# One transfer for wq, narrower last loads for w_up and w_down, and an up-row copy on ScalarE, in a decode layer on one core

## The chip, the cores and the metric

The kernel runs on one core of one Trainium2 chip. TensorE (PE) multiplies matrices, and PEld is its loading of stationary operands. VectorE (DVE) and ScalarE (ACT) do elementwise work, GpSimd (POOL) a little of it, and SyncE (SP) issues the loads. Loads move from device memory into the core's SBUF on 16 DMA engines. The metric is the device time of one execution in microseconds. Before the change it is 294.92 us, the median of three runs from 294.75 to 294.97 us.

## The reference, cut to what matters

Two tokens (batch 2, one position each, width 640) go through one transformer layer: a normalised attention over a cached window, then a gated feed-forward block, each with a residual.

```
x: [2,1,640]   k_cache, v_cache: [2,32,8192,192]   wq: [640,6144]   wo: [6144,640]
W = min(4096, max(256, 8192 // 4))                    # 2048
q = (layernorm(x) @ wq)   as 32 heads of 192
p = softmax(q . k_cache[:, :, 8192-W:, :] * 192**-0.5)
h = x + (p @ v_cache[:, :, 8192-W:, :]) @ wo
h2 = h + (gelu_tanh(layernorm(h) @ w_gate) * (layernorm(h) @ w_up)) @ w_down    # 640 -> 1536 -> 640
```

Everything is bf16 in memory. Only the last 2048 cached positions are read, which is 50.3 MB of K and as much of V, beside 7.9 MB each of wq and wo and 2.0 MB each of w_gate, w_up and w_down.

## The kernel before

**Operations and waits.** The kernel is written as a list of operations in program order. Each names the engine it runs on and the data it reads (`R`), writes (`W`) or shares a PSUM bank in (`X`). A helper then works out the semaphore waits from that list; each engine runs its own operations in exactly the listed order.

**Loads.** All large loads go through `load` and `pump` (L327 to L346) and are issued by SP at L342, in one fixed order: K of group 0, wq, K of group 1, V 0, K 2, V 1, K 3, V 2, K 4 and so on; wo in parts between; and at the end w_gate, w_up and w_down. They share one SBUF buffer, `ring`, of six slots of 24576 bytes per partition. A load may be issued when every earlier load whose bytes it overwrites has been used. SP issues in order, so a load that must wait also holds back those listed behind it. K group g lives in slot g % 4 and V group g in slot 4 or 5. At the start, wq borrows slots that K and V do not need yet: its three loads (`WQC`, 2, 2 and 1 of the five blocks of 128 rows) lie in slot 2, slot 3 and the first half of slot 5 (`WQ_AT`). Thus K 2 waits for the first wq load to be used, V 1 for the third, K 3 for the second; V 0, in slot 4, waits for nothing.

**Attention.** There are 16 groups; a group is four heads of one batch row, 3072 KB of K and 3072 KB of V. For each, TensorE transposes K (`transposes`, L549), DVE and ACT copy the result out (L561, L558), `scores` (L608) multiplies it by the query, `softmax` follows, and `pv` (L652) multiplies the weights by V. The order on TensorE is: transposes of group g, `pv` of group g-1, scores of group g. Before the first scores stand the transposes of K 0, then `q_rows` (L571), which computes the queries in 80 matmuls of 384 columns, 32 on the first wq load, 32 on the second and 16 on the third, then `q_stationary` (L589). After the groups come the last output projections (`oproj`, L703) and the second layer norm.

**Feed-forward.** `ffn_in` (L778) makes the 1536 gate values in 20 matmuls, four row strips of 384 columns side by side; `ffn_columns` copies these rows to `grow` on DVE (L785) and transposes them (L789). `h_rows` (L797) puts the residual into the output bank. DVE and ACT compute the gelu of the gate values (L807 to L814). The same two functions then make the up values from w_up; DVE multiplies both into `uT`; and 48 matmuls (L824), twelve on each of four w_down loads (`WDC`), add the result to the bank. It is copied to `yrow` (L830) and stored by two small transfers (L832).

Of the kernel before, what the change touches and what calls it, by code (L numbers as in the profile page):

```python
# [6 lines left out]
F32 = mybir.dt.float32  # L7
I32 = mybir.dt.int32
ALU = mybir.AluOpType
ACT = mybir.ActivationFunctionType  # L10
# [3 lines left out]
D = 640  # L14
NC5 = D // 128
HQ = 32
DH = 192
SKT = 8192
WIN = 2048
F = 1536  # L20
# [194 lines left out]
SLOT = 24576  # L215
RING = 6 * SLOT
TPG = 64
WQC = ((0, 2), (2, 4), (4, 5))
WDC = ((0, 3), (3, 6), (6, 9), (9, 12))
BIG = 1.0e9  # L220
K_AT = (0, SLOT, 2 * SLOT, 3 * SLOT)
V_AT = (4 * SLOT, 5 * SLOT)
WQ_AT = (2 * SLOT, 3 * SLOT, 5 * SLOT)
WO_AT = (3 * SLOT, 3 * SLOT, 2 * SLOT, 0)
WD_AT = (2 * SLOT + 15360, 2 * SLOT + 19200, 15360, 19200)


def bass_sequential_preLN__sliding_block_cached__geglu_ffn__decode_kernel(
# [12 lines left out]
    with ExitStack() as ctx:  # L241

        def sb(name, shape, dt):
            return ctx.enter_context(nc.sbuf_tensor(name, shape, dt))

        def ps(name, shape, dt):
            return ctx.enter_context(nc.psum_tensor(name, shape, dt))
# [5 lines left out]
        identf = sb("identf", [128, 128], F32)  # L253
# [31 lines left out]
        xnT = sb("xnT", [128, NC5, 136], BF16)  # L285
        hnT = sb("hnT", [128, NC5, B], BF16)
# [21 lines left out]
        hrow = sb("hrow", [128, 320], F32)  # L308
        hsel = sb("hsel", [128, 2, B], F32)
        grow = sb("grow", [128, 384], F32)  # L310
        gsb = sb("gsb", [128, NF * B], F32)
        ga = sb("ga", [128, 4, NF * B], F32)
        uT = sb("uT", [128, NF, B], BF16)

        tps = [ps(f"tps{i}", [128, 512], F32) for i in range(4)]
        sps = ps("sps", [128, 512], F32)
        ops_ = ps("ops", [128, 512], F32)
# [6 lines left out]
        where, live, queue, used = {}, [], [], set()  # L324

        def load(key, off, nbytes, src, shape, sem):
            queue.append((key, off, nbytes, src, shape, sem))  # L327

        def pump():
            while queue:  # L330
                key, off, nbytes, src, shape, sem = queue[0]
                old = [q for q in live if q[1] < off + nbytes and off < q[1] + q[2]]
                if any(q[0] not in used for q in old):
                    return
                for q in old:
                    live.remove(q)
                queue.pop(0)
                live.append((key, off, nbytes))
                v = shape(ring[:, off // 2:(off + nbytes) // 2])
                toks = [("ring", x) for x in range(off // GRAN, (off + nbytes + GRAN - 1) // GRAN)]  # L340
                where[key] = (v, toks)
                P.op("sp", lambda e, v=v, src=src: e.dma_start(v, src), W=toks + [("sem", sem)], dma=sem)  # L342

        def done(*keys):
            used.update(keys)
            pump()  # L346
# [9 lines left out]
            load(("v", g), V_AT[g % 2], SLOT, kv_src(A_v_cache, g), lambda v: v, f"v{g % 4}")  # L356

        def load_wq():
            wq = A_wq.rearrange("(p c) n -> p c n", c=NC5)
            for i, (c0, c1) in enumerate(WQC):  # L360
                load(("wq", i), WQ_AT[i], 2 * (c1 - c0) * HQ * DH, wq[:, c0:c1, :],
                     lambda v: v.rearrange("p (c n) -> p c n", n=HQ * DH), f"wq{i}")

        def load_wo(J):
            src = A_wo[1536 * J:1536 * (J + 1), :].rearrange("(p kk) n -> p kk n", kk=12)
# [5 lines left out]
            return ((0, 12),) if J < 3 else ((0, 8), (8, 12))  # L371

        def load_ffn():
            for key, at, w in (("wg", K_AT[1], B_w_gate), ("wu", K_AT[3], B_w_up)):
                load(key, at, 2 * NC5 * F, w.rearrange("(p c) f -> p c f", c=NC5),
                     lambda v: v.rearrange("p (c f) -> p c f", c=NC5), key)
            wd = B_w_down.rearrange("(r p j) n -> r p j n", p=128, j=3)
            for i, (f0, f1) in enumerate(WDC):
                load(("wd", i), WD_AT[i], 2 * (f1 - f0) * D, wd[i],
                     lambda v: v.rearrange("p (s n) -> p s n", n=D), f"wd{i}")  # L380


        def dve(fn, R=(), W=(), X=(), cls=1):
            return P.op("dve", fn, R, W, X, cls=cls)

        def act(fn, R=(), W=(), X=()):
            return P.op("act", fn, R, W, X)

        def pe(fn, R=(), W=(), X=()):
            return P.op("pe", fn, R, W, X)  # L390
# [10 lines left out]
        def tt(out, a, b, op):  # L401
            return lambda e: e.tensor_tensor(out=out, in0=a, in1=b, op=op)  # L402

        P.op("act", lambda e: e.dma_start(xrow[0:2, :], A_x[:, 0, :]), W=["xrow"], dma="dx")
        load_k(0)
        load_wq()
        load_k(1)
        for g in range(NG):
# [5 lines left out]
        load_wo(2)  # L414
        load_wo(3)
        load_ffn()
        pump()

# [42 lines left out]
        def _x_T(e):  # L461
# [11 lines left out]
            R=["pi"] + [("bits", k) for k in range(11)], W=["pti"])  # L473
# [87 lines left out]
                    dve(lambda e, dst=dst, bv=bv: e.tensor_copy(dst, bv), W=[("kt", n)], X=[("t", bi)], cls=0)  # L561

        def q_rows():
            for i, (c0, c1) in enumerate(WQC):
                wq, wtoks = where["wq", i]

                def fn(e, c0=c0, c1=c1, wq=wq):
                    for c in range(c0, c1):
                        for J in range(4):
                            for r in range(4):  # L570
                                ins = e.matmul(tps[0][32 * r:32 * (r + 1), 0:384], lhsT=xnT[:, c, 32 * J:32 * (J + 1)],  # L571
                                               rhs=wq[:, c - c0, 1536 * J + 384 * r:1536 * J + 384 * (r + 1)],
                                               start=(c == 0 and J == 0), stop=(c == NC5 - 1 and J == 3), tile_position=(0, 32 * r))
                    return ins

                pe(fn, R=["xnT"] + wtoks, X=[("t", 0)])
                done(("wq", i))
            act(lambda e: e.activation(
                out=qrow[:, :, :, :],
                in_=tps[0][:, 0:384].rearrange("p (h d) -> p h d", h=2).unsqueeze(2).to_broadcast([128, 2, 2, DH]),  # L580
                func=ACT.Copy, scale=SCALE), W=["qrow"], X=[("t", 0)])
# [147 lines left out]
        transposes(0, 0)  # L729
        transposes(0, 1)  # L730
        q_rows()
        q_stationary()
        consts_late()
# [35 lines left out]
        layernorm(m2[:, 32:42].rearrange("p (c b) -> p c b", b=B), [], ["m2"], hnT[:, :, :].unsqueeze(2), "hnT",  # L769
                  lambda e: e.matmul(m2[:, 16:18], lhsT=rs[0:98, :].to_broadcast([98, 128]), rhs=bsel[0:98, :], start=True, stop=True))  # L770

        def ffn_in(bank, xt, key):
            wv, wtoks = where[key]

            def fn(e):
                for c in range(NC5):
                    for r in range(4):
                        ins = e.matmul(bank[32 * r:32 * r + 2, 0:384], lhsT=hnT[:, c, :], rhs=wv[:, c, 384 * r:384 * (r + 1)],  # L778
                                       start=(c == 0), stop=(c == NC5 - 1), tile_position=(0, 32 * r))
                return ins  # L780

            pe(fn, R=["hnT"] + wtoks, X=[xt])

        def ffn_columns(bank, xt, i):
            dve(lambda e: e.tensor_copy(grow[0:98, :], bank[0:98, 0:384]), W=["grow"], X=[xt])  # L785

            def fn(e):
                for j in range(3):
                    ins = e.transpose(tps[i][:, 128 * j:128 * j + 98], grow[0:98, j:384:3], identf[0:98, 0:98])  # L789
                return ins  # L790

            pe(fn, R=["grow", "identf"], X=[("t", i)])
            return tps[i][:, 0:384].rearrange("p (j r y) -> p r j y", j=3, y=32)[:, :, :, 0:2]

        def h_rows(e):
            for r in range(4):
# [4 lines left out]
        def rjb(t):  # L801
            return t.rearrange("p (r j b) -> p r j b", r=4, j=3)

        ffn_in(sps, "s", "wg")
        gT = ffn_columns(sps, "s", 0)
        pe(h_rows, R=["hrow", ("hsel", 0), ("hsel", 1)], X=["m1"])
        dve(lambda e: e.tensor_copy(rjb(gsb[:, :]), gT), W=["gsb"], X=[("t", 0)])  # L807
        dve(tt(ga[:, 0, :], gsb[:, :], gsb[:, :], ALU.mult), R=["gsb"], W=["ga0"])
# [3 lines left out]
        dve(ts(ga[:, 3, :], ga[:, 2, :], 1.0, ALU.add), R=["ga2"], W=["ga3"])  # L812
        dve(lambda e: e.reciprocal(ga[:, 1, :], ga[:, 3, :]), R=["ga3"], W=["ga1"])
        dve(tt(ga[:, 0, :], ga[:, 1, :], gsb[:, :], ALU.mult), R=["ga1", "gsb"], W=["ga0"])  # L814
        ffn_in(ops_, "o", "wu")
        vT = ffn_columns(ops_, "o", 1)
        dve(tt(uT[:, :, :].rearrange("p (r j) b -> p r j b", r=4), vT, rjb(ga[:, 0, :]), ALU.mult), R=["ga0"], W=["uT"], X=[("t", 1)])
        for i, (f0, f1) in enumerate(WDC):
            wd, wtoks = where["wd", i]

            def fn(e, f0=f0, f1=f1, wd=wd):
                for f in range(f0, f1):
                    for r in range(4):
                        ins = e.matmul(m1[32 * r:32 * r + 2, 0:160], lhsT=uT[:, f, :],  # L824
                                       rhs=wd[:, f - f0, 160 * r:160 * (r + 1)], start=False, stop=(f == NF - 1),
                                       tile_position=(0, 32 * r), skip_group_check=True)
                return ins
# [3 lines left out]
        for b, q in ((0, "sp"), (1, "act")):  # L831
            P.op(q, lambda e, b=b: e.dma_start(out[b, 0, :].rearrange("(r n) -> r n", r=4), yrow[b:b + 97:32, :]),  # L832
                 R=["y"], W=[("out", b)], dma=f"dout{b}")
# [60 lines left out]
```

## Time and profile before

| what | value |
|---|---|
| median of three runs | 294.92 us |
| the profiled execution | 294.94 us, of which its span from first to last instruction is 293.0 us |
| TensorE busy, weight loads | 198.8 us, 153.0 us |
| VectorE, ScalarE, GpSimd busy | 128.5, 95.7, 8.4 us |
| mean granted TensorE clock | 0.834 of full speed |
| read from memory | 122.29 MB, 417 GB/s over the span |
| share of 16 DMA engines' time taken by SP's loads | 97.8% |
| a K load, issue to landing (median) | 32.7 us |

The span is cut in 40 slices of 7.3 us each for the busy rows. "Releaser" is what ended an engine's wait. A load's time from issue to landing includes the time it stands behind earlier loads.

### The profile page before, as it was taken

The numbers are of one execution on the slowest core, as the hardware profiler recorded it, in microseconds if no ns is written. First come the engines' busy times: TensorE is split into PE (matmuls) and PEld (weight loads), VectorE is DVE, ScalarE is ACT, GpSimd is POOL, SyncE is SP. The second block draws the span as 40 slices with busy tenths as digits, with TensorE's granted clock in tenths as the row PEclk, the third lists the DMA queues.
The fourth block names the chain that finished last, engine by engine and source line by source line (L and its number), as shares of the span: only waits on it lengthen the run. The fifth ranks groups of instructions, "written<-read, shape, count | busy, mean of one in ns | idle before, by whom it ended". The sixth has DMA issues, their size and how long they took to land.

```text
span 293.0 us, 5065 instructions
## 1 busy us (share of the span) xinstructions
PE 198.8 (68%) x2141; PEld 153.0 (52%) x2141; DVE 128.5 (44%) x311; ACT 95.7 (33%) x119; POOL 8.4 (3%) x35
## 2 busy tenths in 40 slices
PE   2573586858677298849493597659696869666764
PEld 1451264838474285628281575356666666533432
DVE  5950364433447045525264155415365435532332
ACT  2150144433442143616161144234343434520000
POOL 3000100000000000000000000000000000000000
PEclk9996569795979579998899599969797968997755
DMA  7999999999999999999999999999999999999993
GB/s 279 436 427 433 431 440 435 430 425 430 425 420 438 430 433 427 430 430 430 430 421 436 430 430 430 430 430 433 430 430 430 430 430 430 430 430 426 430 406 125
DMA packets 6654, 122.44 MB, mean 418 GB/s; under 512 B 754, under 2 KB 756, under 8 KB 1396
## 3 DMA queue, kind: packets, MB, share of 16 engines
q1 hardware_dynamic: 6632, 122.29, 97.8%
q8 instruction: 7, 0.11, 0.2%
q14 instruction: 3, 0.02, 0.0%
q10 hardware_dynamic: 12, 0.00, 0.0%
HBM read 122.29 MB, written 0.00 MB: 417 GB/s over the span
## 4 chain that ended last, share of the span: by engine, by line
DMA 72%; PE 23%; SPq 2%; DVE 2%; issue 1%; ACT 0%
DMA ring<-in_A_k_cache_dram 54%; PE tps L549 16%; DMA ring<-in_A_wq_dram 10%; DMA ring<-in_A_wo_dram 9%; SPq L342 2%; PE ops L652 1%; PE m L703 1%; PE m L824 1%; PE sps L778 1%; PE ops L778 1%; PE m L685 1%; PE tps L789 1%; PE tps L571 1%; PE m L722 0%; DVE grow L785 0%
## 5 line engine op out<-in xcount | busy, mean ns | idle before, releaser
L549 PE MATMUL tps<-identf,ring 128*128 128x128 f32 x768 | 116.5, 320 | 46.4 <-DMA ring<-in_A_k_cache_dram 45.5
L549 PEld LDWEIGHTS tps<-identf,ring 128*128 128x128 f32 x768 | 107.3, 168 | 49.8 <-DMA ring<-in_A_k_cache_dram 46.9
L558 ACT ACTIVATE ktr<-tps 128x1024 bf16<-128x1024 bf16 x80 | 79.4, 1023 | 87.4 <-PE tps L549 87.4
L561 DVE COPY ktr<-tps 128x1024 bf16<-128x1024 bf16 x112 | 74.0, 687 | 74.5 <-PE tps L549 73.8
L627 ACT ACTIVATE eexp<-sm,nm 128x512 bf16<-128x512 f32 x16 | 11.5, 721 | 64.5 <-DVE nm L625 64.5
L652 PE MATMUL ops<-ring,ering 128*32 128x384 bf16 x512 | 24.4, 334 | 4.7 <-DMA ring<-in_A_v_cache_dram 4.7
L608 PE MATMUL sps<-ktr,rq 128*16 128x512 bf16 x384 | 25.9, 404 | 1.1 <-POOL rq L402 1.1
L616 DVE CUSTOM_DVE_ANT_1 sm<-sps,mska 128x512 f32<-128x512 f32 x16 | 11.1, 691 | 34.9 <-PE sps L608 34.9
L652 PEld LDWEIGHTS ops<-ring,ering 128*32 128x32 bf16 x512 | 12.5, 97 | 13.0 <-DMA ring<-in_A_v_cache_dram 6.0
L608 PEld LDWEIGHTS sps<-ktr,rq 128*16 128x16 bf16 x384 | 9.4, 90 | 12.1 <-issue 2.1
L623 PEld LDWEIGHTS m<-mrhs,pm 128*128 128x128 bf16 x16 | 1.5, 96 | 22.8 <-DVE mrhs L398 22.8
L623 PE MATMUL m<-mrhs,pm 128*128 128x16 bf16 x16 | 2.9, 184 | 14.7 <-DVE mrhs L398 14.7
L402 POOL TENSOR_TENSOR rq<-qs,mask 128x96 bf16<-128x96 bf16 x16 | 5.6, 359 | 195.9 <-PE sps L608 164.9
L571 PE MATMUL tps<-ring,xnT 128*32 128x384 bf16 x80 | 5.7, 444 | 7.4 <-DMA ring<-in_A_wq_dram 7.3
L402 DVE TENSOR_TENSOR ering<-m,mask 128x256 bf16<-128x256 f32 x16 | 6.7, 418 | 3.6 <-PE m L636 3.6
L571 PEld LDWEIGHTS tps<-ring,xnT 128*32 128x32 bf16 x80 | 2.4, 120 | 10.3 <-DMA ring<-in_A_wq_dram 8.3
L454 ACT ACTIVATE lt<-m,eps_t 128x2 f32<-128x2 f32 x2 | 0.5, 262 | 20.1 <-PE m L452 20.1
L594 DVE CAST qs<-ops 128x384 bf16<-128x384 f32 x1 | 0.6, 558 | 14.4 <-PE ops L589 14.4
L636 PE MATMUL m<-sel,eexp 128*128 128x64 bf16 x64 | 5.3, 213 | 1.2 <-ACT eexp L627 1.2
L636 PEld LDWEIGHTS m<-sel,eexp 128*128 128x128 bf16 x64 | 4.9, 114 | 1.7 <-DVE nm L625 1.3
L703 PE MATMUL m<-ring,ot 128*2 128x320 bf16 x96 | 4.9, 338 | 1.1 <-DMA ring<-in_A_wo_dram 1.1
L402 DVE TENSOR_TENSOR orow<-m,wm 128x1536 bf16<-128x1536 f32 x3 | 5.3, 1750 | 0.0
(113 smaller groups left out, 84.2 us busy)
## 6 DMA issues: line engine op xcount, KB each, us to landing
ring<-in_A_k_cache_dram SPq DMA_DIRECT2D x16, 3072.0 KB, 32.7
ring<-in_A_v_cache_dram SPq DMA_DIRECT2D x16, 3072.0 KB, 27.6
ring<-in_A_wq_dram SPq DMA_DIRECT2D x2, 3072.0 KB, 21.0
ring<-in_A_wo_dram SPq DMA_DIRECT2D x3, 1920.0 KB, 19.4
ring<-in_B_w_gate_dram SPq DMA_DIRECT2D x1, 1920.0 KB, 30.9
ring<-in_B_w_up_dram SPq DMA_DIRECT2D x1, 1920.0 KB, 27.0
ring<-in_B_w_down_dram SPq DMA_DIRECT2D x4, 480.0 KB, 28.9
ring<-in_A_wq_dram SPq DMA_DIRECT2D x1, 1536.0 KB, 27.9
```

What stands on the lines that cost most here:

```text
L342: P.op("sp", lambda e, v=v, src=src: e.dma_start(v, src), W=toks + [("sem", sem)], dma=sem)
L402: return lambda e: e.tensor_tensor(out=out, in0=a, in1=b, op=op)
L549: ins = e.transpose(tps[bi][:, 128 * u:128 * (u + 1)], kv[:, off:off + 128], identf[:, :])
L558: act(lambda e, dst=dst, bv=bv: e.activation(out=dst, in_=bv, func=ACT.Copy), W=[("kt", n)], X=[("t", bi)])
L561: dve(lambda e, dst=dst, bv=bv: e.tensor_copy(dst, bv), W=[("kt", n)], X=[("t", bi)], cls=0)
L571: ins = e.matmul(tps[0][32 * r:32 * (r + 1), 0:384], lhsT=xnT[:, c, 32 * J:32 * (J + 1)], rhs=wq[:, c - c0, 1536 * J + 384 * r:1536 * J + ...
L608: ins = e.matmul(sps[32 * ch:32 * ch + 16, :], lhsT=rq[:, g % 4, k, :], rhs=ktr[:, k // 2, 1024 * ch + k % 2:1024 * (ch + 1):2], start=(k ...
L616: dve(lambda e: e.tensor_tensor_reduce(out=sm[:, :].rearrange("p (u x) -> p u x", u=4), in0=sps[:, :].rearrange("p (u x) -> p u x", u=4), ...
L627: act(lambda e: e.activation(out=eexp[:, :], in_=sm[:, :], func=ACT.Exp, bias=nm[:, 0:1], scale=1.0, accum_out=zr[:, g % 4:g % 4 + 1]), R= ...
L636: ins = e.matmul(o, lhsT=eexp[:, 128 * u:128 * (u + 1)], rhs=sel64[:, :], start=True, stop=True)
L652: ins = e.matmul(ops_[32 * r:32 * (r + 1), 0:384], lhsT=ering[:, g % 4, t, :], rhs=vv[:, 384 * t:384 * (t + 1)], start=(g % 4 == 0 and t < 4),
L703: ins = e.matmul(m1[32 * r:32 * r + 2, 192:512], lhsT=ot[:, kk, :], rhs=wo[:, kk - k0, 320 * h:320 * (h + 1)], start=(kk == 1 or J < 2 and ...
```

## The change

It has three parts.

- wq comes in one load, with 60 KB (61440 bytes) per partition, at the start of slot 2. It covers slots 2, 3 and the first half of slot 4. `q_rows` is one operation of 80 matmuls that waits for the whole of wq.
- w_up comes in two loads, four of its five blocks and then one (`WUC`), with 16 and 4 matmuls on them; and the last of the four w_down loads becomes two, with 8 and 4 matmuls on them. The bytes stay where they were.
- The rows of up values are copied out of PSUM by ScalarE into a new buffer `urow`; the gate rows stay with VectorE and `grow`.

```diff
-WQC = ((0, 2), (2, 4), (4, 5))
-WDC = ((0, 3), (3, 6), (6, 9), (9, 12))
+WDC = ((0, 3), (3, 6), (6, 9), (9, 11), (11, 12))
+WUC = ((0, 4), (4, 5))
-WQ_AT = (2 * SLOT, 3 * SLOT, 5 * SLOT)
+WQ_AT = 2 * SLOT
-WD_AT = (2 * SLOT + 15360, 2 * SLOT + 19200, 15360, 19200)
+WD_AT = (2 * SLOT + 15360, 2 * SLOT + 19200, 15360, 19200, 19200 + 2560)
...
+        urow = sb("urow", [128, 384], F32)
...
         def load_wq():
-            wq = A_wq.rearrange("(p c) n -> p c n", c=NC5)
-            for i, (c0, c1) in enumerate(WQC):
-                load(("wq", i), WQ_AT[i], 2 * (c1 - c0) * HQ * DH, wq[:, c0:c1, :],
-                     lambda v: v.rearrange("p (c n) -> p c n", n=HQ * DH), f"wq{i}")
+            load("wq", WQ_AT, 2 * NC5 * HQ * DH, A_wq.rearrange("(p c) n -> p c n", c=NC5),
+                 lambda v: v.rearrange("p (c n) -> p c n", n=HQ * DH), "wq")
...
         def load_ffn():
-            for key, at, w in (("wg", K_AT[1], B_w_gate), ("wu", K_AT[3], B_w_up)):
-                load(key, at, 2 * NC5 * F, w.rearrange("(p c) f -> p c f", c=NC5),
-                     lambda v: v.rearrange("p (c f) -> p c f", c=NC5), key)
+            load(("wg", 0), K_AT[1], 2 * NC5 * F, B_w_gate.rearrange("(p c) f -> p c f", c=NC5),
+                 lambda v: v.rearrange("p (c f) -> p c f", f=F), "wg")
+            for i, (c0, c1) in enumerate(WUC):
+                load(("wu", i), K_AT[3] + 2 * c0 * F, 2 * (c1 - c0) * F, B_w_up.rearrange("(p c) f -> p c f", c=NC5)[:, c0:c1, :],
+                     lambda v: v.rearrange("p (c f) -> p c f", f=F), f"wu{i}")
             wd = B_w_down.rearrange("(r p j) n -> r p j n", p=128, j=3)
             for i, (f0, f1) in enumerate(WDC):
-                load(("wd", i), WD_AT[i], 2 * (f1 - f0) * D, wd[i],
+                r = f0 // 3
+                load(("wd", i), WD_AT[i], 2 * (f1 - f0) * D, wd[r][:, f0 - 3 * r:f1 - 3 * r, :],
                      lambda v: v.rearrange("p (s n) -> p s n", n=D), f"wd{i}")
...
         def q_rows():
-            for i, (c0, c1) in enumerate(WQC):
-                wq, wtoks = where["wq", i]
...
-                pe(fn, R=["xnT"] + wtoks, X=[("t", 0)])
-                done(("wq", i))
+            wq, wtoks = where["wq"]
+
+            def fn(e):
+                for c in range(NC5):
+                    for J in range(4):
+                        for r in range(4):
+                            ins = e.matmul(tps[0][32 * r:32 * (r + 1), 0:384], lhsT=xnT[:, c, 32 * J:32 * (J + 1)],
+                                           rhs=wq[:, c, 1536 * J + 384 * r:1536 * J + 384 * (r + 1)],
+                                           start=(c == 0 and J == 0), stop=(c == NC5 - 1 and J == 3), tile_position=(0, 32 * r))
+                return ins
+
+            pe(fn, R=["xnT"] + wtoks, X=[("t", 0)])
+            done("wq")
...
-        def ffn_in(bank, xt, key):
-            wv, wtoks = where[key]
...
+        def ffn_in(bank, xt, key, parts):
+            for i, (c0, c1) in enumerate(parts):
+                wv, wtoks = where[key, i]
+
+                def fn(e, c0=c0, c1=c1, wv=wv):
+                    for c in range(c0, c1):
+                        for r in range(4):
+                            ins = e.matmul(bank[32 * r:32 * r + 2, 0:384], lhsT=hnT[:, c, :], rhs=wv[:, c - c0, 384 * r:384 * (r + 1)],
+                                           start=(c == 0), stop=(c == NC5 - 1), tile_position=(0, 32 * r))
+                    return ins
+
+                pe(fn, R=["hnT"] + wtoks, X=[xt])
...
-        ffn_in(ops_, "o", "wu")
-        vT = ffn_columns(ops_, "o", 1)
+        ffn_in(ops_, "o", "wu", WUC)
+        act(lambda e: e.activation(out=urow[0:98, :], in_=ops_[0:98, 0:384], func=ACT.Copy), W=["urow"], X=["o"])
+        vT = ffn_columns(urow, "urow", tps[1], 1)
```

The gate path keeps its copy on DVE; that copy now stands outside `ffn_columns`, which only transposes.

More of the change, by code (lines that the diff above doesn't have):

```diff
@@ L563, in q_rows @@
         def q_rows():
-            for i, (c0, c1) in enumerate(WQC):
-                wq, wtoks = where["wq", i]
[L567 to L574, printed above, removed]
-                pe(fn, R=["xnT"] + wtoks, X=[("t", 0)])
-                done(("wq", i))
+            wq, wtoks = where["wq"]
[9 more added lines that the diff above has]
+            done("wq")
             act(lambda e: e.activation(
@@ L770, in bass_sequential_preLN__sliding_block_cached__geglu_ffn__decode_kernel, with ffn_columns @@
                   lambda e: e.matmul(m2[:, 16:18], lhsT=rs[0:98, :].to_broadcast([98, 128]), rhs=bsel[0:98, :], start=True, stop=True))
-        def ffn_in(bank, xt, key):
-            wv, wtoks = where[key]
[L775 to L785, printed above, removed]
+        def ffn_in(bank, xt, key, parts):
[8 more added lines that the diff above has]
+                pe(fn, R=["hnT"] + wtoks, X=[xt])
+        def ffn_columns(row, tok, bank, i):
             def fn(e):
                 for j in range(3):
-                    ins = e.transpose(tps[i][:, 128 * j:128 * j + 98], grow[0:98, j:384:3], identf[0:98, 0:98])
+                    ins = e.transpose(bank[:, 128 * j:128 * j + 98], row[0:98, j:384:3], identf[0:98, 0:98])
                 return ins
-            pe(fn, R=["grow", "identf"], X=[("t", i)])
-            return tps[i][:, 0:384].rearrange("p (j r y) -> p r j y", j=3, y=32)[:, :, :, 0:2]
+            pe(fn, R=[tok, "identf"], X=[("t", i)])
+            return bank[:, 0:384].rearrange("p (j r y) -> p r j y", j=3, y=32)[:, :, :, 0:2]
         def h_rows(e):
@@ L802, in rjb @@
             return t.rearrange("p (r j b) -> p r j b", r=4, j=3)
-        ffn_in(sps, "s", "wg")
-        gT = ffn_columns(sps, "s", 0)
+        ffn_in(sps, "s", "wg", ((0, NC5),))
+        dve(lambda e: e.tensor_copy(grow[0:98, :], sps[0:98, 0:384]), W=["grow"], X=["s"])
+        gT = ffn_columns(grow, "grow", tps[0], 0)
         pe(h_rows, R=["hrow", ("hsel", 0), ("hsel", 1)], X=["m1"])
```

## Prediction

> **What bounds the kernel now.** I read the busy rows of the page first, then its chain of work, then the chain in order of time, then the timelines of both ends. The page:
>
> ```profile
> DMA  7999999999999999999999999999999999999993
> ...
> q1 hardware_dynamic: 6632, 122.29, 97.8%
> ...
> DMA 72%; PE 23%; SPq 2%; DVE 2%; issue 1%; ACT 0%
> ```
>
> The DMA row is full in all slices but the first and last: the loads bound the kernel, and a pause in them cannot be made up later. TensorE has room: it waits for K before 14 of the 16 groups (45.5 us in all).
>
> The chain in order of time, at the start:
>
> ```profile
> 2.53 27.89 DMA ring<-in_A_wq_dram
> 30.46 1.50 PE tps L571 x14
> 31.98 0.54 SPq L342
> 32.56 34.38 DMA ring<-in_A_k_cache_dram
> 66.99 5.38 PE tps L549 x24
> ```
>
> The last third of wq lands just before 30.46 us, its 16 matmuls run, and only then SP goes on. The timeline there:
>
> ```profile
> 3.71 0.65 SPq L342 DMA_DIRECT2D ring<-in_A_v_cache_dram  x1
> ...
> 18.96 1.49 PE L571 MATMUL tps<-ring,xnT 128*32 128x384 bf16 x32
> 20.49 0.54 SPq L342 DMA_DIRECT2D ring<-in_A_k_cache_dram  x1
> ...
> 26.77 2.75 PE L571 MATMUL tps<-ring,xnT 128*32 128x384 bf16 x32 [6.32 <-DMA ring<-in_A_wq_dram]
> ...
> 30.46 1.47 PE L571 MATMUL tps<-ring,xnT 128*32 128x384 bf16 x16 [0.95 <-DMA ring<-in_A_wq_dram]
> ...
> 52.38 4.35 PE L549 MATMUL tps<-identf,ring 128*128 128x128 f32 x24 [2.24 <-DMA ring<-in_A_k_cache_dram]
> ```
>
> V 0 is issued at 3.71 and K 2 at 20.49, so when SP is held until 31.98 two or three loads are still queued. K 2 is waited for until 52.38 and K 3 until 66.99, two loads later: 7.3 us per load of 3072 KB. The 32 matmuls took 1.49 us at full clock (46.6 ns each) and 2.75 us at the half clock after 20 us (86 ns each).
>
> The timeline at the end:
>
> ```profile
> 284.26 0.71 PE L797 MATMUL m<-hrow,hsel 98*2 98x160 f32 x8
> ...
> 284.93 0.10 PEld L778 LDWEIGHTS ops<-ring,hnT 128*2 128x2 bf16 x8 [0.56 <-DMA ring<-in_B_w_up_dram]
> ...
> 286.75 0.56 DVE L785 COPY grow<-ops 98x384 f32<-98x384 f32 x1 [0.53 <-PE ops L778]
> ...
> 289.67 0.23 PEld L824 LDWEIGHTS m<-ring,uT 128*2 128x2 bf16 x12 [0.24 <-DMA ring<-in_B_w_down_dram]
> ```
>
> Both waits are short: the arithmetic and the last loads arrive together.
>
> **What the Trainium skill says.** "DMA: Bandwidth & Descriptors", section "Why a DMA increments its semaphore by 16 and not by 1": the engines of a load finish independently, each adding one increment, and only all 16 mean landed. The trace agrees: the increments of wq's third load come at 28.6 to 29.0 us from fourteen engines, at 29.8 and 30.4 from two stragglers; those of K 1 from 35.9 to 37.7, of V 0 from 43.25 to 45.0. "TensorE: Matmul & The Clock Gate", section "What's actually happening": the array runs at half clock until about 3.4 us of sustained work, in a free-running window. Here the transposes ran slow for 3.3 us from 52.38 and for 5.4 us from 66.99.
>
> **Part one, wq.** V 0 lies in slot 4, which wq now covers, so SP waits before V 0 until all 80 query matmuls are done. Behind V 0 on SP stand K 2, V 1, K 3; ahead of it only K 1 is queued. K 1 is 7.3 us of transfer, and in that time the 80 matmuls must end and V 0 be started from an empty queue.
>
> - wq whole: its bytes and place in the stream are unchanged. At worst all increments are there at 30.4 as before; without the later straggler (one of the few instruction fetches, at 23.9 us, sits before it, and may move) at 29.8. I take 30.1.
> - 80 matmuls: TensorE has been idle since 18.9 us, so they begin at half clock. All slow is 80 x 86 ns = 6.9 us. With the clock rising after 3.3 us, 38 are slow and 42 take 46.6 ns: 5.3 us; after 5.4 us, 63 and 17: 6.2 us. I take 5.8. Already-warm would be 3.7. SP then issues about 0.1 us later, at 36.0 (30.1 + 5.8 + 0.1).
> - An unqueued load: K 0 is issued at 0.74, its increments come from 10.32 to 10.75, hence 9.6 to 10.0 us. V 0's first increments come at 36.0 + 9.6 = 45.6, against 43.25: most engines lose 2.35 us. A straggler loses less, 36.0 + 10.0 - 45.0 = 1.0 us.
> - What counts at the end is who finishes last. The increments of w_down's last load come from half the engines by 288.1, from six at 289.1 to 289.3 and from one at 289.6. As only two trailed at wq, most of the six fell back later and carry 2.35 us over: 289.3 + 2.35 = 291.65. The last landing moves by 291.65 - 289.6 = **+2.05 us**.
>
> Later stages shift with the stream. `scores` of group 0 and all behind it start about 4 us later, but `pv(0)` waits for V 0 anyway, and V 2 and K 4, issued after it near 49 us, have K 2, V 1 and K 3 queued ahead to about 68. TensorE's 2.2 to 3.2 us of wait per group take up the rest. One load instead of three saves SP 1.1 us of issuing at 2 us, under K 0's transfer: nothing. Longer rows: I take the same rate, since rows of 24 KB run at the same 430 GB/s as the rest; a per cent of 18.3 us would be 0.2 us either way.
>
> **Part two, w_up and w_down.** `h_rows`' last matmuls start by 284.5 and TensorE could go on at about 284.65, but w_up lands near 284.9. Its first four fifths land 384 KB earlier (0.9 us), and 16 matmuls cover the rest: 0.28 us. For w_down, twelve matmuls from 289.67 take 0.57 us; with a last load of four, all starting together, one matmul's 0.34 us remains: 0.23 us saved after the last landing, of which 44 earlier matmuls must be finished. Two more loads mean two more issues on SP (0.43 us each), at 258 us, when it has idle time until 290, and short rows: I charge 0.05 us. The issue of the last w_down load stood 4.8 us (until 264.5) before; two more such stalls still end well before the data's turn near 287.
>
> **Part three, ScalarE copy.** "ScalarE: Activation LUTs", section "What ACT_TABLE_LOAD costs": 186 ns + 0.833 ns per element, an estimate of 0.51 us for 384. The trace agrees on another tile: 768 elements should be 0.83 us, and L578 took 0.81. DVE took 0.558: 0.05 us saved. ScalarE is idle from 285.45, and the function is one already in use.
>
> **Sum.** w_up and the copy would bring `uT` 0.33 us forward, which only lets the w_down matmuls be ready for the last landing; the gain counted is w_down's 0.23 - 0.05 = 0.2 us. Thus +2.05 - 0.2 = +1.85 us on the profiled execution's 294.94, whose span would be 293.0 + 1.85. It lies 0.02 us from the median, so 294.92 + 1.85 = **296.8 us**.
>
> **Rivals.**
>
> - *Only the stragglers' loss counts* (the pause realigns the engines, and no new lag comes after it): +1.0 - 0.2 = +0.8, 295.7 us. For it: two engines do trail at wq. Against: six others trail at the end. Chance 0.15.
> - *The longer pause*: wq as late as 30.4 and the clock low for all 80: issue at 37.4, 1.4 us later than taken, 298.2 us. For it: in 26.77 to 29.52 and 30.46 to 31.98 the clock stayed at half. Against: transposes never ran slow over 5.4 us. Chance 0.17.
> - *No pause, the tail decides* (the other side): fourteen engines' landing at 29.0 sets the start and the array is warm, 3.7 us, so that V 0 is issued at 32.8, before 43.25 - 9.6 = 33.65. Then the tail's 0.2 to 0.35 us remain, 294.6 us. It is not slower than noise for an issue up to about 34.8 (pause 1.1 us). Against: half clock throughout 25 to 30 us. Chance 0.07.
> - *Mine*: 0.61.
>
> **Numbers.** A change under 0.2% (0.6 us, 294.33 to 295.51) can't be told from none. From the cases: slower 0.90, same 0.08, faster 0.02. The likeliest case alone spans 296.0 to 297.7 (wq 29.8 to 30.4, matmuls 5.3 to 6.2). The range 295.6 to 298.2 takes in the first two rivals and leaves the third out.
>
> **What would show it.** V 0 issued near 36 us after a wait on L571's 80 matmuls, a dent in the DMA row's fifth or sixth slice, K 2 waited for about 1 to 2.5 us later, and K 15 likewise. At the end: no wait before w_up's matmuls, four matmuls after the last landing, a ScalarE copy near 0.5 us. I am wrong if V 0 is issued by 34.5, if wq's landing moves by over 1 us, or if the end keeps less than the pause.

## The result and the profile after

The changed kernel takes 296.43 us (median of five runs, 296.24 to 296.80) against 294.92 us for the kernel before (five runs, 294.54 to 295.04). The ratio is 1.0055, with a 95% interval from 1.004 to 1.007: slower by half a per cent, 1.5 us. The profiled execution took 296.34 us with a span of 294.2 us, against 294.94 and 293.0. The forecast was 296.8 us in a range from 295.6 to 298.2.

**The start.** The timeline of the changed kernel, TensorE and SP (start and duration in us; in square brackets the idle time before and its releaser):

```profile
29.71 4.70 PE L572 MATMUL tps<-ring,xnT 128*32 128x384 bf16 x80 [10.89 <-DMA ring<-in_A_wq_dram]
34.46 0.54 SPq L343 DMA_DIRECT2D ring<-in_A_v_cache_dram  x1
35.03 1.09 SPq L343 DMA_DIRECT2D ring<-in_A_k_cache_dram  x1
...
54.31 1.97 PE L551 MATMUL tps<-identf,ring 128*128 128x128 f32 x8 [3.47 <-DMA ring<-in_A_k_cache_dram]
```

All 80 query matmuls stand in one row after the landing of wq, and SP issues V 0 only behind them, at 34.46 us instead of 3.71. K 2 is now waited for until 54.31 us, 1.9 us later than the 52.38 of before. The waits of SP name the new one: once, for 31.8 us, SP stood until TensorE had done the query matmuls.

```profile
SPq L343 <- PE tps L572: 31.8, 1, 31.8
```

What that does to the stream is seen in windows of 2 us. After the length come the busy times of PE, PEld, DVE, ACT and POOL with their counts of instructions, then the granted clock, the share of the DMA engines and, last, GB/s. The kernel before, then the changed one:

```profile
33.00:35.00 2.00, 0.87 (x16) 0.63 (x18) 1.25 (x5) 0.00 (x0) 0.64 (x2) 0.50 1.08 467
35.00:37.00 2.00, 2.00 (x24) 0.55 (x16) 1.90 (x10) 0.00 (x0) 0.74 (x3) 0.50 0.92 393
37.00:39.00 2.00, 0.92 (x10) 0.29 (x3) 1.46 (x6) 0.00 (x0) 0.35 (x1) 0.50 0.91 393
```

```profile
33.00:35.00 2.00, 1.41 (x36) 0.73 (x28) 0.00 (x0) 0.54 (x1) 0.00 (x0) 1.00 0.97 414
35.00:37.00 2.00, 0.55 (x16) 0.43 (x18) 1.11 (x4) 0.27 (x1) 0.46 (x2) 1.00 0.92 258
37.00:39.00 2.00, 1.52 (x24) 0.48 (x24) 1.90 (x9) 0.00 (x0) 1.28 (x4) 1.00 0.94 393
```

Between 35 and 37 us the changed kernel moves 258 GB/s where the one before moves 393. The share column does not move (0.92 in both). In the packet records the first packets of V 0 took 1.31 to 1.86 us on fourteen engines, where a packet of 24 KB in the full stream takes 0.91, and an engine counts as busy over the whole of such a packet. So here the bytes show the pause and the share does not.

**The end.** The timeline of the changed kernel:

```profile
285.55 0.71 PE L797 MATMUL m<-hrow,hsel 98*2 98x160 f32 x8
...
286.04 1.82 PE L780 MATMUL ops<-ring,hnT 128*2 128x384 bf16 x20
...
287.90 0.49 ACT L817 ACTIVATE urow<-ops 98x384 f32<-98x384 f32 x1 [1.16 <-PE ops L780]
...
290.90 0.10 PEld L826 LDWEIGHTS m<-ring,uT 128*2 128x2 bf16 x8 [0.39 <-DMA ring<-in_B_w_down_dram]
291.30 0.09 PEld L826 LDWEIGHTS m<-ring,uT 128*2 128x2 bf16 x4 [0.29 <-DMA ring<-in_B_w_down_dram]
291.65 0.33 DVE L832 CAST yrow<-m 98x160 bf16<-98x160 f32 x1 [2.22 <-PE m L826]
```

The up matmuls no longer wait for w_up, the ScalarE copy takes 0.49 us, and four matmuls follow the last landing. The chain that ended last, by parts, says the same of the whole. In the kernel before it leads back through wo and the arithmetic behind it, in the changed kernel through w_down's load. The kernel before, then the changed one:

```profile
DMA ring<-in_A_k_cache_dram 54%; PE tps L549 16%; DMA ring<-in_A_wq_dram 10%; DMA ring<-in_A_wo_dram 9%; SPq L342 2%; PE ops L652 1%; PE m L703 1%; PE m L824 1%; PE sps L778 1%; PE ops L778 1%; PE m L685 1%; PE tps L789 1%; PE tps L571 1%; PE m L722 0%; DVE grow L785 0%
```

```profile
DMA ring<-in_A_k_cache_dram 57%; PE tps L551 14%; DMA ring<-in_A_wq_dram 10%; DMA ring<-in_B_w_down_dram 8%; SPq L343 4%; PE tps L572 2%; PE ops L653 1%; DVE ktr L563 1%; ACT ktr L560 1%; PE m L704 1%; PE m L686 1%; DVE ering L404 0%; PE m L826 0%; PE m L667 0%; DVE yrow L832 0%
```

**The increments.** The trace also records each of the 16 increments of a load's semaphore. For V 0 and for the last load of w_down this table gives the first and the last (us); the spread is how far, in the last load, the last engine trails the first. The median time is that of all runs of the kernel, the increments are of its one profiled execution.

```
kernel            V 0 issued   V 0 first   V 0 last   last load: first    last   spread   median time
before               3.71        43.25       45.03        287.50         289.62    2.12      294.92
after               34.46        44.12       45.45        288.52         291.25    2.73      296.43
```

The first engines lose 0.87 us at V 0 and 1.02 us at the end. The last engine loses 1.63 us at the end. The difference of 0.61 us is a spread that has grown. From the last landing to the copy of the output row it was 0.67 us (289.62 to 290.29) and is 0.40 us (291.25 to 291.65), so the new end gives 0.27 us back. The sum is 1.02 + 0.61 - 0.27 = 1.36 us, against 1.40 us between the two profiled executions.

**The engine that lands last.** The packet records do not name the engine, but one engine's packets can be followed, since each begins within 0.02 us of the end of the one before. This is the engine whose V 0 lands last in the changed kernel (us):

```
start            took        size         what
36.90            1.48        24 KB        V 0, its first packet (thirteen other engines begin V 0 by 36.13)
38.38            1.27        24 KB        V 0
39.64 to 49.63   0.91 each   24 KB x11    the rest of V 0, then K 2
49.63            0.94        16 KB        an instruction fetch, on another queue (q8)
50.56            1.42        24 KB        K 2
```

At V 0 this engine trails the first by 1.33 us, where at K 1, just ahead of the pause, the last engine trailed by 1.68: the pause did bring the engines a little closer together. At K 2 it trails by 2.83 us, while the other fifteen lie within 0.75 us. The step of 1.5 us is the fetch and the slower load packet behind it. The kernel before has such a fetch at 49.41 us too, but there it meets one of the fourteen engines that lie within 0.4 us of the first, and the spread stays (1.78 us at V 0, 1.75 at K 2). In the changed kernel's last load, all engines but this one have landed by 290.51 us, 0.89 us after the 289.62 of before. So, by estimate, about 0.7 of the 1.63 us is a fetch that met the engine that was already last.

### The profile page after: what moved, and what is told of

The parts are those of the page before. It is cut to its first block, busy times and chain, and to the rows that moved or that the text cites. A ratio compares the mean times of both kernels' runs of the same rounds, so it can differ in the third digit from the quotient of the medians.

```text
span 294.2 us, 5066 instructions
## 1 busy us (share of the span) xinstructions
PE 193.8 (66%) x2141; PEld 151.1 (51%) x2141; DVE 128.2 (44%) x310; ACT 96.1 (33%) x120; POOL 8.4 (3%) x35
## 4 chain that ended last, share of the span: by engine, by line
DMA 75%; PE 18%; SPq 4%; DVE 1%; ACT 1%; issue 1%
DMA ring<-in_A_k_cache_dram 57%; PE tps L551 14%; DMA ring<-in_A_wq_dram 10%; DMA ring<-in_B_w_down_dram 8%; SPq L343 4%; PE tps L572 2%; PE ops L653 1%; DVE ktr L563 1%; ACT ktr L560 1%; PE m L704 1%; PE m L686 1%; DVE ering L404 0%; PE m L826 0%; PE m L667 0%; DVE yrow L832 0%
## 5 line engine op out<-in xcount | busy, mean ns | idle before, releaser
L551 PE MATMUL tps<-identf,ring 128*128 128x128 f32 x768 | 115.0, 318 | 47.8 <-DMA ring<-in_A_k_cache_dram 46.9
L551 PEld LDWEIGHTS tps<-identf,ring 128*128 128x128 f32 x768 | 106.1, 167 | 51.1 <-DMA ring<-in_A_k_cache_dram 48.2
L653 PE MATMUL ops<-ring,ering 128*32 128x384 bf16 x512 | 25.0, 339 | 4.7 <-DMA ring<-in_A_v_cache_dram 4.7
L617 DVE CUSTOM_DVE_ANT_1 sm<-sps,mska 128x512 f32<-128x512 f32 x16 | 11.1, 691 | 34.8 <-PE sps L609 34.8
L609 PE MATMUL sps<-ktr,rq 128*16 128x512 bf16 x384 | 24.7, 389 | 1.1 <-POOL rq L404 1.1
L572 PE MATMUL tps<-ring,xnT 128*32 128x384 bf16 x80 | 4.7, 407 | 10.9 <-DMA ring<-in_A_wq_dram 10.9
L579 ACT ACTIVATE qrow<-tps 128x768 bf16<-128x768 f32 x1 | 0.8, 810 | 14.6 <-PE tps L572 14.6
```

Of the source, the lines that this page charges most:

```text
L551: ins = e.transpose(tps[bi][:, 128 * u:128 * (u + 1)], kv[:, off:off + 128], identf[:, :])
L609: ins = e.matmul(sps[32 * ch:32 * ch + 16, :], lhsT=rq[:, g % 4, k, :], rhs=ktr[:, k // 2, 1024 * ch + k % 2:1024 * (ch + 1):2], start=(k ...
L617: dve(lambda e: e.tensor_tensor_reduce(out=sm[:, :].rearrange("p (u x) -> p u x", u=4), in0=sps[:, :].rearrange("p (u x) -> p u x", u=4), ...
L653: ins = e.matmul(ops_[32 * r:32 * (r + 1), 0:384], lhsT=ering[:, g % 4, t, :], rhs=vv[:, 384 * t:384 * (t + 1)], start=(g % 4 == 0 and t < 4),
```

## Experiments

The theory: the loss is a pause in the stream of loads, made where V 0 waits for the 80 query matmuls while only K 1 is left in the queue; the end gains a little. All ratios are to the kernel before. The rivals: the one wide load costs by itself; any late use of wq costs; the small loads at the end cost; the loss is partly absorbed.

**The first part alone.** Of the changed kernel only the wq part is kept:

```diff
-WDC = ((0, 3), (3, 6), (6, 9), (9, 11), (11, 12))
-WUC = ((0, 4), (4, 5))
+WDC = ((0, 3), (3, 6), (6, 9), (9, 12))
+WUC = ((0, 5),)
...
-        act(lambda e: e.activation(out=urow[0:98, :], in_=ops_[0:98, 0:384], func=ACT.Copy), W=["urow"], X=["o"])
+        dve(lambda e: e.tensor_copy(urow[0:98, :], ops_[0:98, 0:384]), W=["urow"], X=["o"])
```

> The change with its end undone: wq in one load at slots 2 to 4.5, but w_up in one load, w_down in four, and the up rows copied by VectorE. Pause theory (the whole loss is made at the start, where V 0 waits for the 80 query matmuls): V 0 issued at 34.3 to 35.5 us as in the changed kernel, its first increments near 44.1, and the end keeps it and lacks the 0.2 us of the new end, 296.4 to 297.0 us. Rival (the new small loads at the end cost something): faster than the changed kernel's 296.4, at 295.5 or less.

Measured: 295.99 us (seven runs, 295.46 to 296.74), ratio 1.0033 (1.0022 to 1.0044). The loss is there without the new end. But the median lies below the expected span and below the changed kernel's, and above what the rival asks for. So neither expectation holds as it was put: this kernel lacks the new end and still comes out 0.4 us faster than the changed one, though the intervals of the two ratios overlap. The runs lie 1.3 us apart, where those of the end alone (below) lie 0.5 us apart, so the 0.2 us of the new end cannot be read from this comparison. The profiled execution was the slowest of the seven, with V 0 issued at 35.23 us, as expected; its first increment came at 44.71, later than the 44.1 expected.

**The end alone.** wq, `q_rows`, `WQC` and `WQ_AT` are those of the kernel before:

```diff
+WQC = ((0, 2), (2, 4), (4, 5))
...
-WQ_AT = 2 * SLOT
+WQ_AT = (2 * SLOT, 3 * SLOT, 5 * SLOT)
...
```

> The end alone: wq in three loads as before, w_up in loads of 4 and 1, w_down's last block in 2 and 1, up rows copied by ScalarE. Pause theory: no loss, 0.1 to 0.4 us gained, 294.5 to 294.8 us; w_up's 20 matmuls start without a wait, four matmuls follow the last landing. Rival (small loads and two more issues delay the last landing): 295.2 us or more, with the last landing after 289.8 us.

Measured: 294.75 us (13 runs), ratio 0.9994 (0.9986 to 1.0003). That is within the expected span, but its interval includes no gain. Its one profile has a gain of 0.25 us: the last landing is where it was (289.64 after 289.62), the copy of the output row comes at 290.04 instead of 290.29. The small loads cost nothing that can be seen.

**V slots exchanged.** The one wide load stays, and all 80 query matmuls still wait for all of it; V 0 no longer lies under it:

```diff
-V_AT = (4 * SLOT, 5 * SLOT)
+V_AT = (5 * SLOT, 4 * SLOT)
```

> The changed kernel with the two V slots exchanged (V 0 in slot 5, V 1 in slot 4): wq is still one load of 60 KB rows and all 80 query matmuls still wait for it, but V 0 waits for nothing and K 2 is the first that waits. Pause theory: V 0 is issued near 3 us, K 2 near 34.5 us with V 0 still to come, so the stream has no pause: 294.3 to 294.9 us. Rival (the single wide load, or the late queries, cost the time by themselves): 296.2 to 296.8 us as in the changed kernel.

Measured: 294.54 us (21 runs, 294.22 to 294.93), ratio 0.9988 (0.9981 to 0.9994). This decides between the pause and the wide load. Its timeline of SP at the start and its window from 35 to 37 us:

```profile
2.65 0.60 SPq L343 DMA_DIRECT2D ring<-in_A_v_cache_dram  x1
...
35.78 0.53 SPq L343 DMA_DIRECT2D ring<-in_A_k_cache_dram  x1
```

```profile
35.00:37.00 2.00, 1.08 (x32) 0.61 (x24) 0.00 (x0) 0.81 (x1) 0.00 (x0) 1.00 0.93 393
```

The query matmuls end even later than in the changed kernel (SP goes on at 35.78 us), but it is K 2 that waits then, with V 0 still to be moved, and the stream runs on at 393 GB/s. With the same load and the same late queries the loss is gone, and with it the rival. This kernel is even faster than the kernel before, by 0.12%.

**Queries twice.** The 80 query matmuls are done twice, and the second pass restarts the accumulation:

```diff
-                for c in range(NC5):
+                for c in list(range(NC5)) * 2:
```

> The changed kernel with the 80 query matmuls done twice (the second pass restarts the accumulation, the output is the same). 80 more matmuls at full clock are 3.7 us more before V 0 is issued, near 38.2 us. Pause theory: all of it reaches the end, 299.6 to 300.5 us. Rival (what the start loses is partly absorbed by the 2 to 3 us of room in each group, or by realigned engines): under 298.5 us.

Measured: 299.0 us (four runs, 298.76 to 299.29), 2.6 us over the changed kernel: between the two expectations, so neither holds as it was put. The increments show where the rest went. V 0 is issued 3.89 us later (38.35), its first increment comes 3.68 us later (47.80), and the last load's first 3.73 us later (292.25): the pause reaches the end whole. But the last engine comes only 2.79 us later (294.04), since the spread at the end is 1.79 us instead of 2.73. At V 0 it is 0.48 us (47.80 to 48.28): in the longer pause all engines ran empty, and they restarted together. At K 2 an instruction fetch at 54.23 us puts one of them back, and the spread is 1.91 us; in the changed kernel a fetch in the same load met an engine that was 1.33 us late already. So part of the longer pause is given back, by realigned engines, as the rival said, but only 0.94 of 3.73 us.

**Three loads, but V 0 waits.** wq lies where the changed kernel has it, in three loads:

```diff
+WQC = ((0, 2), (2, 4), (4, 5))
...
-WQ_AT = 2 * SLOT
+WQ_AT = (2 * SLOT, 3 * SLOT, 4 * SLOT)
...
```

> The changed kernel's place of wq (slots 2, 3 and the first half of 4, so V 0 must wait) and its end, but wq again in three loads, with 32, 32 and 16 query matmuls on them. Pause theory: only 16 matmuls stand after the last landing, V 0 is issued near 32.0 us, before the 33.65 us from which a pause begins, so there is none: 294.4 to 295.0 us. Rival (that V 0 waits for wq at all costs the time): 295.8 us or more.

Measured: 294.75 us (13 runs), ratio 0.9996 (0.9988 to 1.0004), V 0 issued at 32.06 us. Waiting for wq costs nothing while the wait ends early enough. It is the 64 matmuls moved behind the last landing that make it late.

**The two halves of the end.** First only w_down's last load is cut, then only w_up is cut and the copy moved to ScalarE; wq is that of the kernel before in both. The diffs are against the kernel with the end alone. The first:

```diff
 WDC = ((0, 3), (3, 6), (6, 9), (9, 11), (11, 12))
-WUC = ((0, 4), (4, 5))
+WUC = ((0, 5),)
...
-        act(lambda e: e.activation(out=urow[0:98, :], in_=ops_[0:98, 0:384], func=ACT.Copy), W=["urow"], X=["o"])
+        dve(lambda e: e.tensor_copy(urow[0:98, :], ops_[0:98, 0:384]), W=["urow"], X=["o"])
```

> The kernel before with only w_down's last load cut in 2 and 1. Theory of the end (it is set by the last landing and the matmuls behind it): four matmuls instead of twelve after the last landing, but they queue behind the eight of the load ahead, so the copy of the output row starts 0.1 to 0.25 us earlier than 290.29; 294.6 to 294.9 us. Rival (the short load lands later): the copy starts at 290.29 or after.

The second:

```diff
-WDC = ((0, 3), (3, 6), (6, 9), (9, 11), (11, 12))
+WDC = ((0, 3), (3, 6), (6, 9), (9, 12))
```

> The kernel before with only w_up in loads of 4 and 1 and the up rows copied by ScalarE. Theory of the end: uT is ready 0.3 us earlier but twelve matmuls still wait for the last w_down load, so the copy of the output row starts within 0.1 us of 290.29; 294.8 to 295.0 us. Rival (the end is set by the chain of arithmetic): 0.3 us gained, 294.6 us, the copy at 290.0.

Measured: 294.77 us, ratio 0.9999 (0.9991 to 1.0007), and 294.88 us, ratio 1.0001 (0.9993 to 1.0009); neither can be told from no change. The timelines show what each does. Only w_down cut:

```profile
288.39 1.77 PE L830 MATMUL m<-ring,uT 128*2 128x160 bf16 x48 [0.28 <-DVE uT L407]
290.21 0.32 DVE L836 CAST yrow<-m 98x160 bf16<-98x160 f32 x1 [1.88 <-PE m L830]
```

Only w_up cut and the copy moved:

```profile
288.00 1.37 PE L830 MATMUL m<-ring,uT 128*2 128x160 bf16 x36 [0.27 <-DVE uT L407]
...
289.81 0.57 PE L830 MATMUL m<-ring,uT 128*2 128x160 bf16 x12 [0.45 <-DMA ring<-in_B_w_down_dram]
290.43 0.33 DVE L836 CAST yrow<-m 98x160 bf16<-98x160 f32 x1 [2.49 <-PE m L830]
```

In the first, the 48 matmuls run without a wait and TensorE is what is late: the copy comes 0.08 us earlier, a little less than expected. In the second, the 36 matmuls start 0.4 us earlier than before (288.00 after 288.40), and the last twelve wait 0.45 us for their load: the copy comes at 290.43, 0.14 us later than before and so just outside the 0.1 us expected, with the last landing 0.15 us later in this execution (289.77). Nothing is gained. By these timelines each half takes away a limit behind which the other stands, and the two together give the 0.25 us; differences as small as these rest on one profile each, and the medians do not resolve them.

**Array kept busy.** 170 matmuls that nothing reads fill TensorE's idle time before wq lands:

```diff
+        def keep_busy(e):
+            for _ in range(170):
+                ins = e.matmul(ops_[:, 0:128], lhsT=identb[:, :], rhs=identb[:, :], start=True, stop=True)
+            return ins
+
+        pe(keep_busy, R=["identb"], X=["o"])
         q_rows()
```

> The changed kernel with 170 matmuls of 128 columns, whose results nothing reads, between the transposes of K 0 and the query matmuls; they fill most of TensorE's idle time until wq lands. Pause theory: the 80 query matmuls then run at full clock, 3.8 us instead of 4.7, V 0 is issued near 33.6 us, at the edge of no pause: 294.6 to 295.3 us. Rival (clock without effect, or the matmuls delay something else): 296.0 us or more.

Measured: 296.3 us (six runs, 295.09 to 296.94), ratio 1.0047 (1.0031 to 1.0063). The expectation failed. Its timeline:

```profile
30.53 3.43 PE L572 MATMUL tps<-ring,xnT 128*32 128x384 bf16 x80 [2.22 <-DMA ring<-in_A_wq_dram]
34.00 0.54 SPq L343 DMA_DIRECT2D ring<-in_A_v_cache_dram  x1
```

At full clock the 80 matmuls take 3.43 us instead of 4.70, but wq lands 0.8 us later (30.39 after 29.57), so V 0 is issued only 0.46 us earlier. The first engines now lose little (V 0 from 43.59 us, 0.34 us late; last load from 287.97, 0.47 us late), yet the last engine ends at 291.06, a spread of 3.09 us, the largest of all. So the first engines' pause is not the whole loss: in this execution most of it is one engine that trails further. Followed through the records, its first packet of V 0 took 2.57 us, and at 151.34 us an instruction fetch of 8 KB met it; the load packet behind that took 1.57 us, and the spread went from 2.32 to 3.25 us.

**A delay in small steps.** To the kernel with three loads in the changed kernel's place, 10 or 30 matmuls that nothing reads are added behind the last landing (shown for 10):

```diff
                 def fn(e, c0=c0, c1=c1, wq=wq):
+                    for _ in range(10 if c1 == NC5 else 0):
+                        e.matmul(ops_[:, 0:128], lhsT=identb[:, :], rhs=identb[:, :], start=True, stop=True)
                     for c in range(c0, c1):
...
-                pe(fn, R=["xnT"] + wtoks, X=[("t", 0)])
+                pe(fn, R=["xnT", "identb"] + wtoks, X=[("t", 0), "o"])
```

> wq in three loads in slots 2, 3 and the first half of 4 (V 0 waits, no pause so far), with 10 matmuls of 128 columns, which nothing reads, put between the landing of the third wq load and its 16 query matmuls: V 0 issued 0.5 to 1.1 us later, near 32.5 to 33.1 us, still before 33.65 us. Pause theory: no cost, 294.5 to 295.0 us. Rival (any wait of V 0 for late queries costs, whether the queue runs dry or not): 295.5 us or more.

> The same with 30 such matmuls: V 0 issued 1.6 to 3.2 us later than without them, near 33.7 to 35.2 us. There is no wide load in it. Pause theory with a straggler on top (an engine that restarts later than the rest): 0.1 to 1.5 us for the first increments and up to 1 us for the last engine, 295.5 to 297.0 us, runs further apart than without a pause. Rival (the loss of the changed kernel needs the one wide load): 294.5 to 295.0 us.

Measured with 10: 294.72 us (13 runs, 294.36 to 295.90), ratio 1.0001 (0.9992 to 1.001), V 0 issued at 33.17 us. With 30: 296.37 us (five runs, 295.80 to 296.75), ratio 1.005 (1.0036 to 1.0064), V 0 issued at 35.25 us. Windows of the second:

```profile
35.00:37.00 2.00, 1.03 (x16) 0.66 (x12) 0.02 (x1) 0.81 (x1) 0.00 (x0) 0.50 0.76 221
37.00:39.00 2.00, 0.93 (x12) 0.37 (x16) 1.93 (x7) 0.00 (x0) 1.37 (x4) 0.50 0.62 246
```

Both times came out as the pause theory had them, with V 0 issued 0.1 us past the spans expected. The same loss arises without any wide load, by delay alone. With the issue at 34.00 us of the kernel with the array kept busy, it begins between 33.2 and 34 us. With 10 matmuls, ten of the 13 runs are at 294.9 or less and three between 295.3 and 295.9, which fits an issue close to the edge.

The kernels whose increments bear on the cause (us); in the first three V 0 does not wait. The increments are those of the profiled execution, whose time is given beside the median:

```
kernel                 V 0 issued   V 0 first   last load: first    last    spread   profiled   median
before                    3.71        43.25        287.50          289.62    2.12     294.94    294.92
end alone                 3.73        43.27        287.67          289.64    1.97     294.78    294.75
V slots exchanged         2.65        43.06        287.41          289.56    2.15     294.62    294.54
three loads, V 0 waits   32.06        43.28        287.66          289.68    2.02     294.86    294.75
10 matmuls more          33.17        43.35        287.75          289.58    1.83     294.36    294.72
array kept busy          34.00        43.59        287.97          291.06    3.09     296.14    296.3
after                    34.46        44.12        288.52          291.25    2.73     296.34    296.43
first part alone         35.23        44.71        288.96          291.38    2.42     296.74    295.99
30 matmuls more          35.25        44.74        289.09          290.81    1.72     295.87    296.37
queries twice            38.35        47.80        292.25          294.04    1.79     298.94    299.0
```

From an issue of about 34 us on, V 0's first increment follows the issue by 9.45 to 9.66 us, and the first engines carry that delay to the end. The spread at the end is 1.8 to 2.2 us in the five kernels without a pause, and in the two with half an end (1.91 and 2.10); it is 1.7 to 3.1 us in the five with a pause.

## Why the prediction was right, and where its working was off

**What held.** The place (V 0 behind all 80 query matmuls), the mechanism (a queue that runs dry) and the threshold: 33.65 us was worked out as the issue from which a pause begins. At an issue of 33.17 us V 0's first increment comes at 43.35, where the kernels in which V 0 does not wait have it (43.06 to 43.36); at 34.00 it comes 0.34 us later than before. K 2 is waited for 1.9 us longer, as was said (1 to 2.5), but only 0.85 us of it is the pause (its first increment at 51.44 after 50.59); the rest is the engine that met the fetch. The two rivals of the range were this mechanism with other sizes. The rival of the other side, no pause at all, is what the exchanged slots show when it is made true: 294.54 us, against its 294.6.

**A sign that came true, and luck.** The prediction calls itself wrong if V 0 is issued by 34.5 us, and it was issued at 34.46. It also took an issue up to about 34.8 for no slower than noise; yet 34.46 cost 1.5 us, and the 34.00 of the kernel with the array kept busy 1.4. With the issue as measured, its own sum gives 34.46 + 9.6 - 43.25 = 0.8 us for most engines, a last landing at 289.3 + 0.8 = 290.1 instead of 289.6, and with 0.2 us off for the end about 295.2 us. This is an estimate, and by the prediction's own limit of 295.51 us it could not be told from no change. So the number came out right in part by luck: an issue taken 1.5 us too late stood in for the engine that trails further, which the sum did not have.

**wq landed: taken 30.1 us, measured 29.57.** The straggler (an engine that lands late) that an instruction fetch made at 23.9 us is gone: the 16 KB packet of that queue comes at 34.8 us in the changed kernel, behind wq. It comes at 33.9 to 34.8 us in all four kernels in which TensorE stands before one wide load, and at 23.1 to 24.0 us in the others, among them the kernel with the array kept busy, where wq's last increment is at 30.39. That TensorE's standing delays the fetch is read from these records, and wasn't tried by itself.

**80 matmuls: taken 5.8 us, measured 4.70.** The term of the sum that was mis-sized most. The clock rose at 32.34 us, 2.6 us after the first matmul, where the two cases in the trace of before (3.3 and 5.4 us) were taken as bounds; that is also less than the about 3.4 us that the prediction cites. Two cases were too few: the matmuls took 5.55 us with the first part alone and 5.95 us with the slots exchanged. With both terms, V 0 was issued at 34.46 us and not at 36.0.

**The unqueued load: taken 9.6 us, measured 9.66.**

**The last landing: +2.05 us forecast, +1.63 measured.** Here the step that failed is 2.35 us for most engines, and 0.3 us taken off for the straggler. The first engines lose 1.02 us, and the last engine trails further (+0.61), where it was to trail less. Two errors of opposite sign left the sum near. The idea itself, realignment, is seen at V 0: from K 1 to V 0 the spread falls from 1.68 to 1.33 us in the changed kernel and from 1.73 to 0.48 us with the queries done twice. What the sum left out is that a later instruction fetch can put an engine back again, here the one that was already last.

**The end: taken 0.2 us, measured 0.27** in the profiles (0.25 for the end alone), and 0.2 us in the medians of the end alone, too little for its interval to exclude no gain. The ScalarE copy took 0.49 us for an estimate of 0.51, and `uT` came forward by more than the matmuls could use, as said.

**Two small slips.** The top of the likeliest case should be 297.5 and not 297.7 us: 30.4 + 6.2 + 0.1 is an issue of 36.7, 0.7 us after the 36.0 taken. And TensorE's waits for K run from 0.8 to 7.4 us in the trace of before, not from 2.2 to 3.2. Nothing in the result turns on either.

**What stays open.** Why engines restart unevenly from an empty queue. In the changed kernel one engine begins V 0 0.8 us after thirteen others; in the first part alone, fifteen engines start V 0 between 36.55 and 37.02 us and one at 38.61, 1.4 us after its own last packet of K 1; with the array kept busy one first packet takes 2.57 us. Nothing recorded explains these delays, and no experiment singled them out. It is open, too, what decides which engine a fetch meets. So of the loss of 1.5 us, about 1.0 us in the profiled execution is the pause, shown by moving V 0's issue both ways. The other 0.6 us is a trailing engine: its late start and the fetch are read from the packet records of this one execution and were not varied. How the loss divides in the other four runs, which have no packet records, is not known.

## What to carry to other kernels

When loads bound a kernel, count for every load what is still queued when it is issued: here K 1's transfer of 7.3 us had to cover the landing's delay, the arithmetic that frees the buffer, and the start from an empty queue. Merging loads moves all the work on them behind the last landing. Here that was free once the next load issued did not need that buffer: exchanging two slots kept the wide load and removed the loss. At an end where arithmetic and the last load arrive together, shorten both: here either alone gained 0.08 us or nothing in its profile. And when a load's last engine decides, ask of that engine by itself what it met.

## What the runs showed of the hardware that was not expected

- At the edge of a pause and just beyond it, runs of one kernel can lie further apart: 1.3 us with the first part alone, 1.5 us with 10 matmuls more and 1.9 us with the array kept busy, against 0.5 us for the end alone and 0.7 us for the exchanged slots. The five runs of the changed kernel lie within 0.6 us, so it is no rule.
- An instruction fetch puts the DMA engine that it meets back, by 1.5 us in the changed kernel: the fetch's packet of 16 KB took 0.94 us, and the load packet behind it 1.42 instead of 0.91.
- An engine that falls behind while the queue is full stays behind. The spread of 2.1 to 2.2 us in the kernel before stands from 152 us to the end; in these traces the spread shrank by more than 0.2 us from one load to the next only at V 0 behind a pause (to 1.33 us in the changed kernel, to 0.48 with the queries done twice).
- The share of busy DMA engines can hide a pause: 0.92 from 35 to 37 us with 258 GB/s in the changed kernel, as with 393 GB/s before.
